# Sliding-window attention and a mixture of experts: the scores in TensorE tiles of 64 rows by 32 columns

## The chip, the core and the metric

The kernel runs on one core of a Trainium2 chip. The metric is device time in microseconds (us) of one execution. Before the change the median of three runs is 652.78 us (652.28 to 653.83). One execution was also taken by the hardware profiler: its own time is 656.34 us, and its span, from the first to the last instruction of the profile, is 654.3 us.

## What is computed

Attention with a causal window of 64 positions feeds a layer of eight experts, of which each token uses one. Cut to what matters here:

```python
B, H, S, D = 8, 8, 576, 64          # batch, heads, positions, head width; all float32
scores = q @ k.T / sqrt(D)          # per batch and head
rel = pos[:, None] - pos[None, :]
mask = (rel >= 0) & (rel < 64)      # a query sees itself and the 63 keys before it
attn = softmax(where(mask, scores, -1e9))
x = attn @ v                        # heads side by side: (B, S, 512)
...
e = argmax(x @ w_gate)              # or the expert of the position before, by a local gate
out = p[e] * (relu(x @ w1[e]) @ w2[e])
```

## The kernel before, in words

The 8 x 576 = 4608 positions are one row of tokens, cut into nine superblocks of 512 (`SC`, index `sc`). Heads are taken in pairs: `hp` counts four pairs, and `j` the two heads of a pair. A pair of `sc` and `hp` is a unit; there are 36, worked through in order.

Queries and keys lie with the 64 channels of a head on the partitions, head `j` on partitions 64j to 64j+63. Scores are made transposed: keys on the partitions of PSUM, queries along the columns. Keys come in blocks of 64. A PSUM bank (128 partitions by 512 float32) holds the scores of one head for the 512 queries of the unit: even key blocks in partitions 0 to 63 (`c` = 0), odd ones in 64 to 127 (`c` = 1). The 64 keys of a block can be seen by 128 queries, those of the block itself and of the next, so each matmul takes 64 keys as its stationary operand and streams 128 queries (64 at the two ends): `scores`, L376 to L420, with the matmul itself at L383. A unit has 18 such matmuls: in each head four even blocks of 128 queries, three odd ones of 128 and two odd ends of 64. Row half (head) and column half (`c`) make four tiles of 64 by 64 in TensorE's array. In the profile a float32 matmul is two weight loads (PEld, LDWEIGHTS) and two MATMUL records: 648 matmuls give 1296 of each.

ScalarE takes the exponential of the bank (L414) into an SBUF tile `p`, and VectorE multiplies it with a mask of zeros and ones (L419). In five of the 36 units (`BIASED`) there is no mask; instead small bfloat16 matmuls (L398) first write large negative numbers where a query doesn't see a key, and the score matmuls add to them (`start=False`). The banks come from a pool of three, `ps_s`, two for a unit.

`values` (L422 to L440) multiplies `p` with the values, in matmuls of 128 keys by 64 queries (L429), with a column of ones for the sum, and VectorE divides by that sum (L434, L439). Beside these, TensorE turns the results of some superblocks (L300) and computes gate logits (L313, L315, L330). A router works out the tables of the experts step by step between units (`step()`), on VectorE above all.

What sets the order: TensorE, ScalarE and SyncE run attention in the order in which the program writes it down (`manual_schedule`, L202). Scores are issued two units ahead of the values (`LEAD`, L475 and L501). SyncE (SP) issues the loads: queries and keys of a superblock (2 MB, L231) go into a ring of four 2 MB buffers, which is shared with the experts' weights (L1143), values (1.0 to 1.2 MB, L226) and, in the last five superblocks, values turned (1 MB, L221) go into buffers of their own. Loads are for the superblock after next, and each waits for its buffer to be released. GpSimd writes each superblock's result to DRAM (L529), some 1 MB. After attention the experts' stage runs to the end: gathered rows, two products per expert block (L1212, L1260, L1351, L1383) and scattered results, with small blocks in tiles of 128 by 32 (L1303, L1320).

Of the kernel before, what the change touches and what calls it, by code (L numbers as in the profile page):

```python
# [8 lines left out]
F32 = mybir.dt.float32  # L9
# [7 lines left out]
PSUM = bass.MemoryType.PSUM  # L17
DRAM = bass.MemoryType.DRAM

P = 128  # L20
B, H, S, DH = 8, 8, 576, 64
# [2 lines left out]
DK, FK = D // P, F // P  # L24
WIN = 64
KW = P + WIN
N = B * S
C = N // P
GB = 2
# [14 lines left out]
assert CUT and CUT % 32 == 0  # L44
LEFT = N - FB * BIG
HF = P // 2
NB = (N + E * (HF - 1)) // BIG
SM0 = NB * 2
# [10 lines left out]
SC = 4 * P  # L59
NSC = N // SC  # L60
HP = H // 2
KB = SC // WIN
# [19 lines left out]
def kernel(  # L82
# [20 lines left out]

    xs = dram.tile([N + 2, D], F32, name="xs")
    lt = const.tile([P, C, E + 1], F32, name="lt")
# [16 lines left out]
    with ExitStack() as fast:  # L122
        ring = fast.enter_context(tc.tile_pool(name="ring", bufs=4))
        rt = Router(fast, tc, lt, tabs, ident)
        ex = Experts(fast, tc, ring, *moe)
        zrow = ex.xp.tile([P, D], F32, name="xg")[:1]
        nc.vector.memset(zrow, 0.0)
        for i in (ZR, N + 1):
            nc.gpsimd.dma_start(out=xs[i:i + 1, :], in_=zrow)
        attention(tc, ring, kq, v3, v4, vt, vh, xs, lt, ok, wgs, wg2s, ident, rt, ex)  # L130
        ex.run(fast, rt, lambda ps: flag(nc, ps, ok, bad, tabs["ej"][:, NBLK:], rare, ident))
# [34 lines left out]
def attention(ctx, tc, ring, kq, v3, v4, vt, vh, xs, lt, ok, wg, wg2, ident, rt, ex):  # L166
# [14 lines left out]
    nc = tc.nc  # L181
# [3 lines left out]
    pp = ctx.enter_context(tc.tile_pool(name="at_p", bufs=LEAD + 3))  # L185
    wk = ctx.enter_context(tc.tile_pool(name="at_work", bufs=2))

    ps_s = ctx.enter_context(tc.tile_pool(name="at_ps_s", bufs=3, space=PSUM))
    ps_e = ctx.enter_context(tc.tile_pool(name="at_ps_e", bufs=1, space=PSUM))

    ps_x = [ctx.enter_context(tc.tile_pool(name=f"at_ps_x{i}", bufs=1, space=PSUM)) for i in range(2)]
# [8 lines left out]
        return ps_e.tile([P, SC], F32, name="r")  # L200

    ctx.enter_context(tc.manual_schedule(engines={ET.PE, ET.Activation, ET.SP}))  # L202

    kqs, qts, kts, vts, vas, vbs = {}, {}, {}, {}, {}, {}

# [169 lines left out]

    def scores(sc, hp):  # L376
        qt, kt = qts[sc], kts[sc]
        sp = [ps_s.tile([P, SC], F32, name="sp") for _ in range(2)]
        biased = (sc, hp) in BIASED

        def one(j, c, kt, block, a, b):
            h = slice(j * DH, (j + 1) * DH)
            nc.tensor.matmul(sp[j][c * WIN:(c + 1) * WIN, a:b], lhsT=kt[h, hp, block * WIN:(block + 1) * WIN],  # L383
                             rhs=qt[h, hp, a:b], start=not biased, stop=True, skip_group_check=biased)

        first = -sc * KB % SB
        if biased:
            for n in range(2):
                for c in range(2):
                    for j in range(2):  # L390
                        h, a = slice(j * DH, (j + 1) * DH), slice(0, SC)
                        x = bias[h, c].rearrange("p b i q -> p (b i q)")
                        if n:

                            if first >= KB or c == first % 2:
                                continue
                            a, x = slice(first * WIN, (first + 1) * WIN), never[h]
                        nc.tensor.matmul(sp[j][c * WIN:(c + 1) * WIN, a], lhsT=unit[h], rhs=x, start=not n, stop=False,  # L398
                                         skip_group_check=True)
        for s in range(5):  # L400
            for c in range(2):
                for j in range(2):
                    if c == 0:
                        if s < 4:
                            one(j, 0, kt, 2 * s, s * P, (s + 1) * P)
                    elif s:
                        one(j, 1, kt, 2 * s - 1, s * P - WIN, min(s * P + WIN, SC))
                    elif sc:
                        one(j, 1, kts[sc - 1], KB - 1, 0, WIN)
                    else:  # L410
                        one(j, 1, kt, 1, 0, WIN)
        p = pp.tile([P, 2, SC], F32, name="p")
        for j in range(2):
            nc.scalar.activation(p[:, j], sp[j], Act.Exp, scale=DH ** -0.5)  # L414
        if biased:
            return p
        a = 0 if sc == KB else (MID[sc % 2] - sc) * WIN
        m = masks[sc % 2][:, a:a + SC].rearrange("p (o x) -> p o x", o=1)
        masked.append(nc.vector.tensor_tensor(p, p, m.to_broadcast([P, 2, SC]), op=Alu.mult))  # L419
        return p  # L420
# [24 lines left out]
    for u in units[:LEAD]:  # L445
        ps[u] = scores(*u)
# [22 lines left out]
    for i, (sc, hp) in enumerate(units):  # L469
# [5 lines left out]
        if 1 < i < len(units) - LEAD:  # L475
            ps[units[i + LEAD]] = scores(*units[i + LEAD])
# [24 lines left out]
        if i < 2:  # L501
            ps[units[i + LEAD]] = scores(*units[i + LEAD])
# [32 lines left out]
    f = wk.tile([P, SC], F32, name="gs", bufs=1)[:, :NSC * 4 * H]  # L535
# [6 lines left out]
def careful(ctx, tc, q, k, v, xs, lt, wgs, ident):  # L542
# [15 lines left out]
    for cross in (False, True):  # L558
        m = cp.tile([P, 2, KW], F32, name=f"mask{int(cross)}")
        nc.gpsimd.memset(m, 0.0)  # L560
        nc.gpsimd.affine_select(out=m, in_=m, compare_op=Alu.is_ge, fill=NEG, base=-1,
                                pattern=[[0, 2], [1, KW]], channel_multiplier=-1)
        nc.gpsimd.affine_select(out=m, in_=m, compare_op=Alu.is_ge, fill=NEG, base=WIN,
                                pattern=[[0, 2], [-1, KW]], channel_multiplier=1)
        if cross:
            u = m[WIN:, :, :]
            nc.gpsimd.affine_select(out=u, in_=u, compare_op=Alu.is_ge, fill=NEG, base=-P,
                                    pattern=[[0, 2], [1, KW]], channel_multiplier=0)
        masks.append(m)
# [16 lines left out]
    def scores(st, half):  # L586
# [3 lines left out]
        for i in range(2):  # L590
            for j in range(2):
                h = slice(j * DH, (j + 1) * DH)
                nc.tensor.matmul(sp[:, j, i * KW + lo:(i + 1) * KW], lhsT=qt[h, 2 * half + i, t0:t0 + P],
                                 rhs=kt[h, 2 * half + i, t0 - WIN + lo:t0 + P], start=True, stop=True)
        s = wk.tile([P, 2, 2, KW], F32, name="s")
        mask = masks[st["c"] == CROSS]
# [938 lines left out]
```

## Time and profile before

| quantity | value |
|---|---|
| median of three runs | 652.78 us (652.28 to 653.83) |
| the profiled execution: its time, its span | 656.34 us, 654.3 us |
| PE busy, share of the span | 625.4 us, 96% |
| weight loads (PEld) busy | 538.5 us, 82% |
| VectorE, ScalarE, GpSimd busy | 402.2, 182.6, 124.4 us |
| records of PE and of PEld | 6307 each |
| score matmuls (L383): records, mean duration of one | 1296, 271 ns |
| value matmuls (L429): records, mean duration of one | 1152, 230 ns |
| exponentials (L414): count, mean | 72, 595 ns |
| first and last start of a score matmul | 5.3 and 133.9 us |
| data moved by DMA | 165.78 MB, mean 253 GB/s |

How to read it: PE rows are matmuls, PEld rows the loads of their stationary operand; both are TensorE. Matmuls are pipelined and last longer than the step from one to the next, so their busy times overlap, and the distance between starts says more than the duration. "Idle before" is time in which an engine stood still ahead of an instruction, with what ended the wait; "issue" there means that the profile knows of no wait. In the slices of the span each digit is the busy share of a fortieth of it (16.4 us), in tenths. The DMA queue that is called "instruction" brings the engines' instructions; the others carry data.

### The profile page before, as it was taken

To read this page: it belongs to the slowest core of one execution; us is meant where nothing else is said; L and a number is where in the kernel's file an instruction comes from. 1 tells how busy PE (TensorE), PEld (TensorE's weight loads), DVE (VectorE), ACT (ScalarE), POOL (GpSimd) and SP (SyncE) were. 2 spreads that over 40 slices of the span, in tenths; PEclk is the share of its full clock that TensorE was granted. 3 is DMA by queue.
4 is the path that set the end of the run, shared out by engine and by line. 5 is a ranking of instruction groups with operands and counts; after the bars stand their busy time and mean duration, and the time that the engine had idled before them with its cause. 6 is when DMAs were issued, how large, how long until landed. Compare 5 with 4: busy or idle time off the path is not lost. (4 is left out here: it accounts for less than half of the span.)

```text
span 654.3 us, 14680 instructions
## 1 busy us (share of the span) xinstructions
PE 625.4 (96%) x6307; PEld 538.5 (82%) x6307; DVE 402.2 (61%) x742; ACT 182.6 (28%) x318; POOL 124.4 (19%) x131
## 2 busy tenths in 40 slices
PE   8889887999999999999999999999999999999996
PEld 7777765786666899988799799978987998999994
DVE  5676479783996758336290876182835663876730
ACT  2866654621111221203121122113120322123220
POOL 5222111330104111121220311031222111101001
PEclk9999999999999999999999999999999999999998
DMA  9979989997436547566967845686858655945601
GB/s 337 400 292 395 362 311 361 371 357 277 161 128 216 204 160 262 204 218 248 374 244 264 310 174 185 263 304 264 339 183 307 241 198 180 386 165 190 245 17 39
DMA packets 21999, 165.78 MB, mean 253 GB/s; under 512 B 3453, under 2 KB 4483, under 8 KB 11940
## 3 DMA queue, kind: packets, MB, share of 16 engines
q1 hardware_dynamic: 13108, 135.24, 56.7%
q0 software_dynamic: 8816, 29.50, 11.4%
q8 instruction: 52, 0.85, 0.5%
q14 instruction: 23, 0.19, 0.1%
HBM read 145.85 MB, written 19.27 MB: 252 GB/s over the span
## 5 line engine op out<-in xcount | busy, mean ns | idle before, releaser
L1333 POOL DMA_INDIRECT out_dram<-y,idx x36 | 40.4, 1123 | 312.8 <-DVE y L1269 127.9
L1212 PE MATMUL hp<-xs,ws 128*128 128x128 f32 x672 | 79.7, 275 | 1.0 <-issue 1.0
L1212 PEld LDWEIGHTS hp<-xs,ws 128*128 128x128 f32 x672 | 77.3, 192 | 1.2 <-issue 1.2
L1260 PE MATMUL hp<-ws,hs 128*128 128x256 f32 x336 | 77.6, 380 | 0.0
L1260 PEld LDWEIGHTS hp<-ws,hs 128*128 128x128 f32 x336 | 63.5, 190 | 9.3 <-issue 0.8
L1351 PE MATMUL hp<-xt,w 128*64 128x64 f32 (+2 forms) x640 | 65.9, 275 | 0.0
L1269 DVE SCALAR_TENSOR_TENSOR y<-hp,pw,kept 128x256 f32<-128x256 f32 x42 | 19.7, 482 | 73.1 <-issue 48.7
L1351 PEld LDWEIGHTS hp<-xt,w 128*128 128x128 f32 (+1 forms) x640 | 60.8, 170 | 4.6 <-issue 1.1
L1223 DVE TENSOR_TENSOR h<-hp,keep 128x512 f32<-128x512 f32 x42 | 28.6, 690 | 54.0 <-PE hp L1212 46.7
L1131 POOL DMA_INDIRECT xg<-xs,gx x40 | 45.5, 1137 | 84.2 <-PE tp L1157 70.7
L1383 PE MATMUL yp<-w,h 128*128 128x512 f32 x128 | 56.2, 592 | 0.0
L1212 PEld LDWEIGHTS hp<-xt,w 128*128 128x128 f32 x448 | 53.2, 192 | 2.7 <-issue 1.3
L1212 PE MATMUL hp<-xt,w 128*128 128x128 f32 x448 | 54.7, 275 | 0.0
L1260 PE MATMUL hp<-w,h 128*128 128x256 f32 x224 | 53.6, 382 | 0.0
L419 DVE TENSOR_TENSOR p<-p,mask 128x1024 f32<-128x1024 f32 x31 | 39.1, 1265 | 20.7 <-ACT p L414 20.6
L414 ACT ACTIVATE p<-sp 128x512 f32<-128x512 f32 x72 | 39.1, 595 | 41.2 <-PE sp L383 39.1
L383 PEld LDWEIGHTS sp<-w 64*64 64x64 f32 x1296 | 38.7, 138 | 14.1 <-issue 10.7
L429 PE MATMUL xo<-vb,p 128*64 128x74 f32 (+1 forms) x576 | 44.8, 230 | 4.2 <-ACT p L303 1.5
L383 PE MATMUL sp<-w 64*64 64x128 f32 (+1 forms) x1296 | 44.2, 271 | 4.5 <-issue 3.6
L429 PE MATMUL xo<-va,p 128*64 128x74 f32 (+1 forms) x576 | 44.6, 230 | 3.4 <-DVE va L346 3.3
L429 PEld LDWEIGHTS xo<-vb,p 128*64 128x64 f32 x576 | 38.9, 138 | 8.5 <-issue 3.9
L1260 PEld LDWEIGHTS hp<-w,h 128*128 128x128 f32 x224 | 41.3, 190 | 5.6 <-issue 0.4
(284 smaller groups left out, 935.8 us busy)
## 6 DMA issues: line engine op xcount, KB each, us to landing
w<-in_w_dram SPq DMA_DIRECT2D x48, 2048.0 KB, 9.0
w<-in_kq_dram SPq DMA_DIRECT2D x17, 1024.0 KB, 10.5
xs<-x POOLq DMA_DIRECT2D x9, 1024.0 KB
va<-in_v_dram SPq DMA_DIRECT2D x5, 1184.0 KB
vtt<-in_vt_dram SPq DMA_DIRECT2D x5, 1024.0 KB, 6.7
va<-in_v_dram SPq DMA_DIRECT2D x3, 1040.0 KB, 8.0
va<-in_v_dram SPq DMA_DIRECT2D x2, 520.0 KB, 6.9
w<-in_kq_dram SPq DMA_DIRECT2D x2, 512.0 KB, 3.9
```

The lines of the kernel that those rows point to most:

```text
L383: nc.tensor.matmul(sp[j][c * WIN:(c + 1) * WIN, a:b], lhsT=kt[h, hp, block * WIN:(block + 1) * WIN], rhs=qt[h, hp, a:b], start=not biased, ...
L414: nc.scalar.activation(p[:, j], sp[j], Act.Exp, scale=DH ** -0.5)
L419: masked.append(nc.vector.tensor_tensor(p, p, m.to_broadcast([P, 2, SC]), op=Alu.mult))
L429: nc.tensor.matmul(xo[par * WIN:(par + 1) * WIN, j, s * VW:s * VW + n], lhsT=p[:, j, b * WIN:(b + 1) * WIN], rhs=w[:, s, 2 * hp + j, :n], ...
L1131: self.nc.gpsimd.indirect_dma_start(out=x, out_offset=None, in_=self.xs[:rows, :], in_offset=bass.IndirectOffsetOnAxis(ap=gx[:, s:s + 1], ...
L1212: nc.tensor.matmul(out[:, m, :], lhsT=a[:, kk, m * P:(m + 1) * P], rhs=b[:, kk, :], start=start and m + kk == 0, stop=stop and (m, kk) == ...
L1223: nc.vector.tensor_tensor(o, x, y, op=add)
L1260: nc.tensor.matmul(out, lhsT=a[:, m, :], rhs=b[:, m, :], start=start and m == 0, stop=stop and m == FK // 2 - 1, skip_group_check=True)
L1269: nc.vector.scalar_tensor_tensor(y[i][:, j * w:(j + 1) * w], x, pw[i], y2, Alu.mult, Alu.add)
L1333: self.nc.gpsimd.indirect_dma_start(out=self.out[:, :], out_offset=bass.IndirectOffsetOnAxis(ap=st["idx"][:, s:s + 1], axis=0), in_=y, in_ ...
L1351: nc.tensor.matmul(hp[a, i, :], lhsT=st["w1"][:, kk, m * P:(m + 1) * P][:, a], rhs=st["xt"][:, kk, :n], start=(kk == 0), stop=(kk == DK - 1))
L1383: nc.tensor.matmul(yp, lhsT=st["h"][:, m, i * P:(i + 1) * P], rhs=st["w2"][:, m, :], start=(m == 0), stop=(m == FK - 1))
```

## The change

The score matmuls are cut finer. The 64 keys of a block become two halves of 32 (`half`), each a matmul of its own into a tile of 64 rows by 32 columns. The first 32 keys of a block are seen by its own 64 queries and the first 32 of the next block, the other 32 from the 32nd query of their block on: each matmul now streams 96 queries in place of 128 (64 and 32 at the ends). A unit has 36 score matmuls in place of 18, in eight tiles in place of four. Part of each bank is then never written by a score matmul: those places hold scores that the mask sets to zero anyway. So that they hold finite numbers, the three banks are made once, zeroed by VectorE at the start, and taken in turn by `bank_s()`, in place of being allocated from the pool for each unit. The bias matmuls (L398), the exponential, the mask and the values are as before.

```diff
+HW = WIN // 2
...
-    ps_s = ctx.enter_context(tc.tile_pool(name="at_ps_s", bufs=3, space=PSUM))
+    ps_s = ctx.enter_context(tc.tile_pool(name="at_ps_s", bufs=1, space=PSUM))
...
+    sps = [ps_s.tile([P, SC], F32, name=f"sp{i}") for i in range(3)]
+    for sp in sps:
+        nc.vector.memset(sp, 0.0)
+
+    def bank_s():
+
+        sps.append(sps.pop(0))
+        return sps[-1]
...
-        sp = [ps_s.tile([P, SC], F32, name="sp") for _ in range(2)]
+        sp = [bank_s() for _ in range(2)]
         biased = (sc, hp) in BIASED
 
-        def one(j, c, kt, block, a, b):
-            h = slice(j * DH, (j + 1) * DH)
-            nc.tensor.matmul(sp[j][c * WIN:(c + 1) * WIN, a:b], lhsT=kt[h, hp, block * WIN:(block + 1) * WIN],
-                             rhs=qt[h, hp, a:b], start=not biased, stop=True, skip_group_check=biased)
+        def one(j, c, half, kt, block, own):
+
+            h, r = slice(j * DH, (j + 1) * DH), half * HW
+            q = slice(max(own + r, 0), min(own + r + WIN + HW, SC))
+            nc.tensor.matmul(sp[j][c * WIN + r:c * WIN + r + HW, q],
+                             lhsT=kt[h, hp, block * WIN + r:block * WIN + r + HW], rhs=qt[h, hp, q],
+                             start=not biased, stop=True, skip_group_check=biased)
...
         for s in range(5):
             for c in range(2):
-                for j in range(2):
-                    if c == 0:
-                        if s < 4:
-                            one(j, 0, kt, 2 * s, s * P, (s + 1) * P)
-                    elif s:
-                        one(j, 1, kt, 2 * s - 1, s * P - WIN, min(s * P + WIN, SC))
-                    elif sc:
-                        one(j, 1, kts[sc - 1], KB - 1, 0, WIN)
-                    else:
-                        one(j, 1, kt, 1, 0, WIN)
+                for half in range(2):
+                    for j in range(2):
+                        if c == 0:
+                            if s < 4:
+                                one(j, 0, half, kt, 2 * s, s * P)
+                        elif s:
+                            one(j, 1, half, kt, 2 * s - 1, s * P - WIN)
+                        else:
+                            one(j, 1, half, *((kts[sc - 1], KB - 1) if sc else (kt, 1)), -WIN)
```

## The prediction, as it was made

> **What bounds the kernel now.** I read the slices first. TensorE looks full in attention, its clock is granted in full, and the DMA engines are nearly full over the first seven slices (to about 115 us); later they are not.
>
> ```profile
> PE   8889887999999999999999999999999999999996
> ...
> PEclk9999999999999999999999999999999999999998
> DMA  9979989997436547566967845686858655945601
> ```
>
> Attention's steady stretch, 12 to 139 us, in the view by stages (columns: busy us of PE, PEld, DVE, ACT, POOL with record counts, clock, DMA share, GB/s):
>
> ```profile
> 12.00:139.00 127.00, 111.87 (x2635) 91.16 (x2633) 94.21 (x238) 74.43 (x126) 29.60 (x38) 0.99 0.93 353
> ```
>
> PE is busy 112 of 127 us; no other engine comes near. So PE's own work counts, but so do its 15 us of gaps. The waits of the score line say what ended its idle time, matmuls and weight loads together:
>
> ```profile
>   issue: 14.3, 15
>   ACT p L414: 2.4, 4
> ```
>
> "Issue" means that nothing the profile knows held the engine. The timeline shows such gaps in the middle of one unit's scores, where the next matmuls need no new data:
>
> ```profile
> 28.43 0.65 PE L383 MATMUL sp<-w 64*64 64x128 f32 x12
> 29.78 0.99 PE L383 MATMUL sp<-w 64*64 64x128 f32 x24 [0.70 <-issue]
> ...
> 75.64 1.09 PE L383 MATMUL sp<-w 64*64 64x128 f32 x28
> 78.55 0.55 PE L383 MATMUL sp<-w 64*64 64x128 f32 x8 [1.82 <-issue]
> ```
>
> I then numbered PE's records (weight loads and matmuls together). The gaps that no wait explains fall at numbers 705, 961, 1217, 2753, 3009, 4801 and 5313, all 193 plus a multiple of 256. They last 0.74, 0.70, 0.92, 0.15, 1.82, 1.08 and 0.34 us, 5.75 us in all. So it is the arrival of PE's instructions, in pages of 256. The page lists that queue (packets, MB, share of 16 engines):
>
> ```profile
> q8 instruction: 52, 0.85, 0.5%
> ```
>
> 0.85 MB over 52 packets is 16 KB each, 64 bytes for each of 256 instructions; 52 x 256 = 13,312 covers PE's 2 x 6307 records. By the single records, each page of attention has one such packet, lasting 0.9 to 1.7 us (mostly 1.0), and after every one of the seven gaps PE resumes 1.3 to 1.6 us after its end. The packet comes late: PE entered a page at 22.89 us, the packet for the next began at 27.33, ended at 28.40, and PE, out of instructions at 28.82, went on at 29.78. Taking a page's entry as the later of its arrival and the start of the record 64 earlier (the queue ahead of the array, see below), the wait from entry to packet in 20 pages averages 4.1 us in 17 (2.8 to 5.4), when loads were queued, and 1.1 to 1.4 us in three, when few or none were. So from request to use: 4.1 + 1.0 + 1.4 = **6.5 us** among loads, about 1.2 + 2.4 = **3.6 us** without. The stretch crosses 20 pages in 127 us, 6.35 us each, and by these times 13 of 20 pages arrived later than the queue could have taken them up. PE's instruction supply is a second bound, as tight as its matmuls.
>
> **What the Trainium skill says.** "Runtime: NRT & Kernel Launch", section "Instruction fetch mechanics": instruction memory is refilled in 16 KiB blocks of 256 instructions, the sequencer fetching the next while it executes the current one, and the crossing is mostly hidden. The trace agrees on the block and on one block ahead, and not on hidden: 5.75 us of gaps. "DMA: Bandwidth & Descriptors", section "Queues, rings and completion order": each DMA engine takes turns between queues, a packet at a time, so a fetch shares engines with loads; the 4.1 against 1.2 us fit. "TensorE: Matmul & The Clock Gate", section "Architectural detail": PE's queue holds 64 instructions; a gap shows only once it is empty, which fits that gaps are shorter than the lateness. "TensorEngine Tiling (Array Packing)", "Tiling Modes": 64x32 gives eight tiles that load and multiply independently, and changing the mode drains the array. No row has 64x32, but 128x32 with four tiles runs at full stream, and tiles start 7 ns apart:
>
> ```profile
> 318.20 1.95 PE L1320 MATMUL yp<-w,qt 128*32 128x128 f32 x64
> ```
>
> (64 passes over four tiles, 16 each, steps of 109 ns: 1.75 us and an end.)
>
> **The change, part by part.**
>
> *Fewer columns.* A float32 matmul is two passes, each a weight load and a matmul record (648 matmuls, 1296 records of each). In one tile the passes of 128 columns step by 109 ns, those of 64 by 56; 96 columns lie midway, 82 ns. A tile's eight passes of 128 (512 columns) become eight of 96: 8 x 27 = 0.21 us saved a unit, 7.7 us in 36 units. Eight tiles at 7 ns between starts need 56 ns a round, under 82, so the starts fit. If 64x32 doesn't stream so, this gain goes, and up to the present 0.90 us of a unit may double.
>
> *Twice the instructions.* Each unit issues 36 matmuls for 18, hence 72 weight loads and 72 passes for 36 and 36. In the stretch 1224 records of each kind belong to scores (34 units); 2448 are added to 5268: 7716, 30.1 pages for 20.6. Nothing else on PE is removed.
>
> *What that does to supply.* Work left per page is (111.9 - 7.3) / 30.1 = 3.5 us, against 5.4 now. A page among loads takes 6.5 us, so PE runs dry in nearly each. Loads occupy 44.9 MB (353 GB/s x 127 us) at some 395 GB/s, the rate of full slices: 113 us, however long the stretch is, since SP issues them when PE frees a buffer (SP's longest wait is for PE's L429, 40 us). During them 113 / 6.5 = 17.4 pages pass. The other 12.7 take the larger of 3.6 and 3.5 plus drains, 3.8 us: 48 us. The stretch becomes 161 us. The same sum on the kernel before gives 17.4 pages in 113 us and 3.2 at 5.4: 130 us against 127 measured. I take the difference of the two sums and the difference to the trace, 31 and 34, as +33 us. It already contains the 7.7 us: they shorten work that is no longer late.
>
> *Banks and zeros.* Three memsets of 512 columns on DVE; one such row takes 0.48 us, so they end near 2.9 us, ahead of the first scores at 5.33; ACT's table load, which now waits for them, ends near 4.2, ahead of the first exponential at 7.40. Nothing. Without that cover 1.4 us, once. The turn of three banks is the pool's own. In the five biased units the bias matmuls are 64x64 and the scores 64x32: five more drains of about 0.1 us, under the fetches.
>
> *Bounds and the rest.* If fetch delays among loads fall to 5.4 us since loads lie further apart, 113 / 5.4 = 20.9 pages and 9.2 x 3.8 = 35: 148 us, +18 to +21. If PE's clock halves in its idle spells (the trace has 0.83 in the stage 80 to 90 us, after the 1.82 us gap), the quiet pages cost 5.2: +18 us more. Later work keeps its length: first expert weights land about 14 us ahead of use, and from 139 us PE has 64 of 66 us busy.
>
> **Sum.** The profiled execution took 656.34 us (span 654.3), 3.6 over the median 652.78. 656.34 + 33 = 689; on the median 652.78 + 33 = 686; with a little for the clock, **687**.
>
> **Rivals.** (a) *Supply stays hidden* and the columns decide: 7.7 less 0.5 for drains, **645.6**. For it: most crossings show no visible gap. Against: pages come just in time now. It decides if a page among loads arrives within about 3.5 us. (b) *Two pages are requested at once* when PE runs dry, so delays overlap: a page costs (3.0 + 6.5) / 2 = 4.8, 23.5 pages in 113 us and 6.6 at 3.6: 137, +7 to +10, **661**. Against: after visible gaps the next packet comes 1.3 to 4.9 us after the resumption; counted from the last instruction before the gap it would be up to 6, longer than in the other pages. (c) *Starts limit eight tiles*: pairs no closer than today's 25 ns average make a unit 1.8 us. With fetches over much of it: **700**. Against: the 7 ns.
>
> **How the numbers follow.** Forecast 0.78 (668 to 710 by the bounds), (a) 0.07, (b) 0.10, (c) or a halved clock 0.05. The range 662 to 712 leaves out (a), half of (b) and the tails. A change of 0.2% is about what can be told here. Faster is (a): 0.07; same 0.02; slower 0.91.
>
> **What would show it.** Right: the instruction queue has 62 packets for 52; "issue" gaps of 1 to 4 us every 256 PE records in attention; PE busy share of the early slices falls to 5 or 6; loads get quiet spells; the stretch is some 33 us longer, the rest unchanged. Score passes stepping 82 ns with eight tiles shows the first part right. Wrong: as many gaps as now, or score units without gaps that last 1.3 us or more.

## The result, and the profile after

| | before | after |
|---|---|---|
| median of four runs, us | 652.53 (652.22 to 653.83) | 694.25 (691.42 to 696.60) |
| ratio, 95% interval | | 1.063 (1.060 to 1.066) |
| profiled execution: time, span, us | 656.34, 654.3 | 691.42, 689.6 |
| attention's stretch, us | 126.4 | 161.6 |
| TensorE records in the stretch, in pages of 256 | 5261, 20.6 | 7679, 30.0 |
| page gaps over 0.3 us: number, sum in us | 7, 7.5 | 18, 37.9 |
| TensorE at half clock in the stretch, us | 3.4 | 44.4 |

The stretch is counted here, and for all kernels below, from 12 us to the first TensorE record of the experts' first product (L1351 before, L1363 after; it is a wait, 0.7 us ahead of the first matmul). TensorE's records are its matmuls, its weight loads and its waits for semaphores, in the order of their starts. A page gap is the distance between the starts of two neighbouring records at a number of 193 plus a multiple of 256, if over 0.3 us.

The change costs 41.7 us in the medians and 35.1 us between the two profiled executions. The spans differ by 35.3 us, the stretches by 35.2. So the whole of what the profiles show was lost in attention, and 30.4 us of it are page gaps (37.9 for 7.5). The other 4.8 us aren't located. What follows it kept its length and its work, as the view by stages says of the kernel before (columns: stretch of time, its length, then busy us of PE, PEld, DVE, ACT, POOL with record counts, clock, DMA share, GB/s),

```profile
139.00:654.00 515.00, 504.42 (x3586) 439.07 (x3582) 302.50 (x493) 103.91 (x187) 88.69 (x79) 1.00 0.62 228
```

and of the kernel after, its attention first:

```profile
12.00:173.60 161.60, 122.67 (x3823) 98.59 (x3823) 90.81 (x236) 74.06 (x125) 29.99 (x38) 0.86 0.74 281
...
173.60:689.00 515.40, 504.81 (x3606) 439.66 (x3602) 302.71 (x494) 104.21 (x188) 86.05 (x79) 1.00 0.61 227
```

In the first line PE has 39 us without work where it had 15, its clock is 0.86 for 0.99, and the DMA engines, full before, stand still for a quarter of the time. The slices of the page show the same against the kernel before: PE's first ten digits fall from 7 to 9 to 6 to 8, the clock has dents among them, and the loads have quiet spells.

```profile
PE   7677777868999999999999999999999999999995
...
PEclk9689999898999999999999999999999999999998
DMA  9668777785835375556696676566966674854601
...
q8 instruction: 62, 1.02, 0.6%
```

The instruction queue brought 62 pages in place of 52. What ended the idle time ahead of the score matmuls, in the view of that line (us in all, times; the idle times of PE and PEld are added, so that most gaps count twice):

```profile
  issue: 60.6, 39
  ACT p L426: 3.0, 4
```

It was 14.3 us. The timeline shows where: in the middle of one unit's scores, which need nothing new. Columns are start, duration, instruction, count, and the idle time before it.

```profile
15.73 0.68 PE L395 MATMUL sp<-w 64*32 64x96 f32 x34
19.98 1.17 PE L395 MATMUL sp<-w 64*32 64x96 f32 x40 [3.57 <-issue]
...
151.69 0.37 PE L395 MATMUL sp<-w 64*32 64x96 f32 x12
156.27 1.49 PE L395 MATMUL sp<-w 64*32 64x64 f32 x60 [4.21 <-issue]
```

Both gaps stand at a page's border by the count of records. The packet of the missing page can be read beside them: the one for the second gap was asked for at 148.97 us, began 5.0 us later and lasted 0.9, and PE went on 1.4 us after it ended.

The zeroing of the banks, which the prediction priced at nothing, lies where it was put. ScalarE's table load waits for the first of the three banks and is done at 3.4 us, ahead of the first scores at 5.3:

```profile
1.57 1.57 DVE L207 MEMSET sp<- 128x512 f32 x3
2.14 1.28 ACT L426 ACT_TABLE_LOAD   x1 [2.14 <-DVE sp L207]
```

### The profile page after: what moved, and what is told of

It reads as the page before. It is cut to its first block, busy times and chain, and to the rows that moved or that the text cites. A ratio compares the mean times of both kernels' runs of the same rounds, so it can differ in the third digit from the quotient of the medians.

```text
span 689.6 us, 17285 instructions
## 1 busy us (share of the span) xinstructions
PE 636.3 (92%) x7603; PEld 546.2 (79%) x7603; DVE 401.4 (58%) x745; ACT 182.6 (26%) x318; POOL 121.9 (18%) x131
## 5 line engine op out<-in xcount | busy, mean ns | idle before, releaser
L1345 POOL DMA_INDIRECT out_dram<-y,idx x36 | 38.7, 1076 | 311.4 <-DVE y L1281 128.1
L395 PE MATMUL sp<-w 64*32 64x96 f32 (+2 forms) x2592 | 47.8, 265 | 25.5 <-issue 24.3
L395 PEld LDWEIGHTS sp<-w 64*32 64x32 f32 x2592 | 39.8, 117 | 39.7 <-issue 36.3
L1363 PE MATMUL hp<-xt,w 128*64 128x64 f32 (+2 forms) x640 | 65.9, 275 | 0.0
L1363 PEld LDWEIGHTS hp<-xt,w 128*128 128x128 f32 (+1 forms) x640 | 60.8, 170 | 4.6 <-issue 1.1
L441 PE MATMUL xo<-vb,p 128*64 128x74 f32 (+1 forms) x576 | 50.3, 247 | 9.6 <-issue 4.2
L441 PEld LDWEIGHTS xo<-vb,p 128*64 128x64 f32 x576 | 44.2, 153 | 17.4 <-issue 13.7
L441 PE MATMUL xo<-va,p 128*64 128x74 f32 (+1 forms) x576 | 50.1, 247 | 2.1 <-issue 2.1
```

The source lines that it names most:

```text
L395: nc.tensor.matmul(sp[j][c * WIN + r:c * WIN + r + HW, q], lhsT=kt[h, hp, block * WIN + r:block * WIN + r + HW], rhs=qt[h, hp, q], start=n ...
L441: nc.tensor.matmul(xo[par * WIN:(par + 1) * WIN, j, s * VW:s * VW + n], lhsT=p[:, j, b * WIN:(b + 1) * WIN], rhs=w[:, s, 2 * hp + j, :n], ...
L1345: self.nc.gpsimd.indirect_dma_start(out=self.out[:, :], out_offset=bass.IndirectOffsetOnAxis(ap=st["idx"][:, s:s + 1], axis=0), in_=y, in_ ...
L1363: nc.tensor.matmul(hp[a, i, :], lhsT=st["w1"][:, kk, m * P:(m + 1) * P][:, a], rhs=st["xt"][:, kk, :n], start=(kk == 0), stop=(kk == DK - 1))
```

## The experiments

Two theories were held against each other. *Supply*: the added instructions make TensorE wait for its instruction pages, which come slowly while loads are moving. *Array*: eight tiles of 64 by 32 load and multiply slower than four of 64 by 64, and the time is lost inside a unit's scores. In e2, e3, e8 and e12 scores are missing or others than asked for. This changes the routing, extra paths of the program then run, and their total times of 1016 to 1059 us say nothing. Only attention's stretch is used of them; the total times that were expected of e2 and e3 can't be compared. e8, e9 and e12 were executed once each. The stretch varies from execution to execution: kernels that keep the instruction count of before give 122.7 to 126.4 us.

| kernel | stretch, us | TensorE records, pages | page gaps: number, us | at half clock, us | time over before |
|---|---|---|---|---|---|
| e1: 64x64, queries cut in two | 156.5 | 7138, 27.9 | 14, 28.1 | 27.3 | 1.049 (1.044 to 1.054) |
| e2: 64x32, half of the keys | 126.4 | 5256, 20.5 | 8, 12.5 | 10.2 | |
| e3: 64x64, one head of two | 120.3 | 4032, 15.8 | 2, 3.0 | 6.8 | |
| e4: banks alone | 122.7 | 5197, 20.3 | 9, 8.8 | 3.4 | 1.003 (1.001 to 1.005) |
| e5: after, loads in 2 KB | 165.8 | 7671, 30.0 | 22, 42.7 | 41.0 | 1.060 (1.054 to 1.066) |
| e6: before, loads in 2 KB | 126.1 | 5215, 20.4 | 7, 6.5 | 10.2 | 1.004 (1.002 to 1.005) |
| e8: after, half of the q and k loads | 155.6 | 7644, 29.9 | 16, 33.6 | 27.3 | |
| e9: after, loads in 16 KB | 163.2 | 7622, 29.8 | 18, 38.0 | 41.0 | one run: 692.76 us |
| e10: before, 18 small matmuls a unit more | 163.5 | 7341, 28.7 | 13, 23.2 | 20.5 | 1.059 (1.051 to 1.067) |
| e11: before, 9 small matmuls a unit more | 143.1 | 6325, 24.7 | 12, 11.1 | 3.4 | 1.030 (1.024 to 1.035) |
| e12: after, 8 queries a matmul | 163.9 | 7686, 30.0 | 19, 41.2 | 68.3 | |
| e13: before, 72 empty instructions a unit more | 267.3 | 7821, 30.6 (2492 of them empty) | 0 | 97.5 | 1.214 (1.209 to 1.219) |

### Tile shape or instruction count: e1 and e2

e1 keeps the kernel before with its tiles of 64 by 64 and cuts each score matmul of 128 queries in two:

```diff
-            nc.tensor.matmul(sp[j][c * WIN:(c + 1) * WIN, a:b], lhsT=kt[h, hp, block * WIN:(block + 1) * WIN],
-                             rhs=qt[h, hp, a:b], start=not biased, stop=True, skip_group_check=biased)
+            for q in range(a, b, WIN):
+                nc.tensor.matmul(sp[j][c * WIN:(c + 1) * WIN, q:q + WIN],
+                                 lhsT=kt[h, hp, block * WIN:(block + 1) * WIN],
+                                 rhs=qt[h, hp, q:q + WIN], start=not biased, stop=True, skip_group_check=biased)
```

> The kernel before, with its tiles of 64 by 64 and all its columns, but each score matmul of 128 queries is cut into two of 64: 32 matmuls a unit in place of 18, the columns the same. Attention's stretch then has 5268 + 34 x 56 = 7172 instructions on TensorE, 28.0 pages. Theory of instruction supply: the changed kernel took 39 us more for 9.5 pages more, 4.1 us a page, so 7.4 pages more cost 30 us: 683 us (675 to 690), with unexplained gaps at every 256th record. Rival, that tiles of 64 by 32 themselves are slow: no such tile here, so 652 to 658 us. Rival, that only columns count: 652.5 to 654 us.

Measured: 687.66 us, 1.049 times before; the stretch is 156.5 us. No tile is finer than before, no column is added, and yet 30 of the 35 us are there. The finer cut has an array cost of its own, though: a unit without a gap takes 1.204 us from first to last start (29.78 to 30.98 here),

```profile
29.78 1.42 PE L384 MATMUL sp<-w 64*64 64x64 f32 x64
```

and 0.900 before (14.68 to 15.58):

```profile
14.68 1.12 PE L383 MATMUL sp<-w 64*64 64x128 f32 x36
```

In 34 units that is up to 10 of the 30 us. The page gaps grew by 20.6 us. e2 is the other half, the changed kernel with the first 32 keys of each block alone, so that the old instruction count meets the new tiles:

```diff
-                for half in range(2):
+                for half in range(1):
```

> The changed kernel, but only the first 32 keys of each block are multiplied (half = 0); the other half of the scores is left out, and those places keep zeros or the bias. 18 matmuls a unit, as many instructions as the kernel before, all in tiles of 64 by 32 with 96 queries. Supply theory: 20.6 pages in the stretch as before, and 0.2 us less work a unit that mostly only widens the gaps: 650 us (644 to 654). Rival, that the tile shape is slow: the shape is used in every unit, so half of the loss or more stays: 670 us or more.

Measured: a stretch of 126.4 us, equal to before. Together they say that the time goes with the count more than with the tiles. e2 has half of the matmuls, in four tiles at a time, so it doesn't tell how eight tiles work together; the units of the changed kernel itself do, under e12.

### Fewer instructions, and the banks alone: e3 and e4

Both take from the change only the banks that are made once and zeroed. e3 also leaves out the scores of the second head (`for j in range(1)` in the loop of the score matmuls).

> The kernel before with its three banks made once and zeroed, and the score matmuls of the second head of each pair left out (its banks keep what was in them). The two tiles that are left still stream 512 columns each, so the array is occupied as long as before, with half the score instructions: 5268 - 1224 = 4044 in the stretch, 15.8 pages. Supply theory, that already the kernel before is held by its pages: the gaps of 5.75 us go and late pages hold nothing: 645 us (641 to 648). Rival, that the kernel before is bound by its columns alone and supply bound only the changed one: 651.5 to 653.5 us.

Measured: 15.8 pages in place of 20.6, two page gaps for seven, and a stretch that is 6 us shorter than before. e3 has the banks of e4, though, and against e4 it is 2.4 us shorter, less than the 3.7 us by which kernels of one count differ. That the kernel before lost a little to its supply is seen in its own seven gaps; what their absence gains e3 doesn't show.

> One part of the change alone: the three banks made once, zeroed at the start and taken in turn, with the matmuls of the kernel before. All theories: nothing, 652.5 us (651.5 to 653.5). If the turn of the banks or the memsets had a share in the loss, it would show here.

Measured: 656.11 us, 1.003 (1.001 to 1.005), a little above the expected range. The profiled execution doesn't contain the difference (its span of 652.2 us is 2.1 below the one of before), so it isn't located. It is at most 3 us of the 41.7.

### The same count with little to multiply: e12

The changed kernel, each score matmul cut to its first 8 queries; most scores are left out.

```diff
-            q = slice(max(own + r, 0), min(own + r + WIN + HW, SC))
+            q = slice(max(own + r, 0), max(own + r, 0) + 8)
```

> The changed kernel with each score matmul cut from 96 queries to the first 8: the same 36 matmuls a unit in the same eight tiles, so the same instruction count, with a twelfth of the streaming. Most scores are left out, so the routing is another and only attention's stretch is to be compared. Theory (count and supply decide): 157 to 162 us, as the changed kernel's 161.6, with as many late pages. Rival (the array's work in eight tiles costs the time): the stretch falls by what a unit's scores shrink, 34 x 0.3 to 0.5 us = 10 to 17 us, to 145 to 151 us.

Measured: 163.9 us, as the changed kernel. Whole units without a gap show that the array's work did shrink. A unit's scores after,

```profile
32.94 1.07 PE L395 MATMUL sp<-w 64*32 64x96 f32 x72
```

and in e12:

```profile
53.86 0.78 PE L395 MATMUL sp<-w 64*32 64x8 f32 x72
```

From first to last start, a clean unit (no gap, full clock) takes 0.612 us and not 0.867; in 34 units that is 8.7 us of array work less, and nothing of it shows in the stretch. What ended the idle time ahead of e12's score line is almost what it was after:

```profile
  issue: 57.7, 42
```

The stretch of e12 alone doesn't refute the array theory. e12 ran 68 us at half clock, 24 more than the changed kernel, and that can have made up for the 8.7 us: by the prediction's rule for a page's entry, TensorE didn't wait for 7 of its 30 pages, and five of these 7 follow a page worked through mostly at half clock. So e12 doesn't settle either what the half clock was worth.

Two readings of the changed kernel decide. Its 16 clean units of scores take 0.867 us each, where a clean one took 0.900 before: in eight tiles a unit is no slower, and there is nothing for the array theory to explain. And by the same rule 26 of its 30 pages (13 of 20 before) began only when their packet had come, at every gap 1.2 to 1.6 us after the packet's end.

### Count added to the kernel before: e10, e11 and e13

e10 sends ahead of each score matmul, in units without bias, one of 8 queries into the same place; e11 does so for the first head alone (`if not biased and j == 0`).

```diff
         def one(j, c, kt, block, a, b):
             h = slice(j * DH, (j + 1) * DH)
+            if not biased:
+                nc.tensor.matmul(sp[j][c * WIN:(c + 1) * WIN, a:a + 8], lhsT=kt[h, hp, block * WIN:(block + 1) * WIN],
+                                 rhs=qt[h, hp, a:a + 8], start=True, stop=True)
```

> The kernel before (64x64 tiles, 128 queries), with an added matmul of 8 queries ahead of each score matmul, whose result the score matmul overwrites; in the 31 units without bias matmuls. That is the instruction count of the changed kernel almost in full (some 7350 in the stretch, 28.7 pages) with next to no array work added. Theory (count of instructions, supplied among loads at 6.5 us a page and else at 3.8): 17.4 pages in 113 us and 11.3 x 3.8 = 43 us, 156 us by the sum that gave 130 for the 126 to 127 us of before: a stretch of 152 to 156 us, time 678 to 684 us. Rival (the array's work in eight finer tiles costs the time): 127 to 130 us and 653 to 656 us.

> The same with the added matmuls for the first head of each pair alone: half of the added instructions (some 6300 in the stretch, 24.6 pages). Theory: 17.4 pages in 113 us and 7.2 pages at their own work of 4.55 us, 33 us: 146 by the sum, 142 to 146 in the trace, time 668 to 673 us. Rival (there is slack up to some count, and only the full count goes beyond it): 127 to 132 us, time 653 to 658 us.

Measured: 694.17 and 672.54 us, stretches of 163.5 and 143.1. (One of e10's four executions took 1768 us, for a cause that no trace shows. The ratio leaves it out; the other three took 689.9 to 695.4 us.) e10 overshot its expectation, and its units show why that can be: from first to last start a clean one takes 1.736 us and in e11 1.628, for 0.900 before. The small matmuls were not next to nothing; each brings two weight loads and two passes more. Over 29 units that is 24 us in e10 and 21 in e11, where the stretches grew by 37 and 17 and the page gaps by 15.7 and 3.6. e10 and e11 therefore don't separate the theories. e11's hit on the number of the supply theory is no support for it.

e13 wanted the added count with no array work: four empty instructions ahead of each score matmul, 2592 in all, as many as the change adds.

```diff
         def one(j, c, kt, block, a, b):
             h = slice(j * DH, (j + 1) * DH)
+            for _ in range(4):
+                nc.tensor.nop(hint="keep", nofuse=True)
```

> The kernel before with four empty instructions (no operation) on TensorE ahead of each score matmul: 2592 added in attention, exactly as many as the change adds, and no work on the array at all. Theory (count and supply): the stretch becomes 152 to 162 us, time 678 to 694 us, the instruction queue has 62 packets, and the late pages come every 256 instructions with the empty ones counted. Rival (array work in finer tiles): 126 to 130 us and 652 to 656 us. Second rival (the empty ones are slow by themselves): the time is lost inside each unit of scores and not at the pages.

Measured: 794.8 us. The second rival of its expectation is what happened. A unit's scores last up to 5.59 us, and none of the 30 page borders in the stretch shows a gap:

```profile
22.10 5.59 PE L385 MATMUL sp<-w 64*64 64x128 f32 x36
```

The same 36 passes lasted 1.12 us before. The empty instructions have records, too: 2592 of them, two thirds of which start 70 or 71 ns after the one before. A page then lasts 8.7 us on average, and the next one has all the time it needs. The run confirms one number only: its instruction queue brings 62 packets, as after, so empty instructions fill pages as others do.

### Why a page takes so long: e5, e6, e9 and e8

The prediction had the fetch wait for load packets on a shared DMA engine. If it is packets that it waits for, their size must matter. e5 cuts the loads of the changed kernel into rows of 2 KB for queries and keys (8 KB before), and the values likewise; e6 does the same to the kernel before; e9 loads queries and keys in rows of 16 KB, from the second superblock on.

```diff
-                nc.sync.dma_start(out=vts[sc], in_=vt[GATED.index(sc)])
+                for hp in range(HP):
+                    nc.sync.dma_start(out=vts[sc][:, hp], in_=vt[GATED.index(sc)][:, hp])
...
-                nc.sync.dma_start(out=vas[sc][:, :, h], in_=src[:, :, h])
+                for c in range(4):
+                    nc.sync.dma_start(out=vas[sc][:, c, h], in_=src[:, c, h])
...
-                nc.sync.dma_start(out=kqs[sc][:, part], in_=kq[sc, :, part])
+                for hp in range(part.start, part.stop):
+                    for i in range(2):
+                        nc.sync.dma_start(out=kqs[sc][:, hp, i], in_=kq[sc, :, hp, i])
```

> The changed kernel with its loads of queries, keys and values cut finer: queries and keys in rows of 2 KB and not of 8 KB in one partition, values per four-way chunk, turned values per head pair; the same bytes, more DMAs, the same TensorE instructions. Theory (an instruction page waits behind a number of load packets already queued on its DMA engine, whose size sets the wait): the wait from request to packet among loads falls from about 3.8 us towards 2 us, the attention stretch from 162 us to 130 to 140 us, the time to 660 to 675 us. Rival (the wait is set by bytes in flight, or by something other than the loads): the wait stays near 3.8 us, the stretch near 160 us and the time near 694 us. Second rival (the added issues on SP delay the loads themselves): ScalarE and TensorE waits for loads appear and the time is above 694 us.

> The kernel before with the same finer loads. Theory (wait behind load packets): its seven page gaps of 7.5 us vanish and the time falls to 645 to 649 us. Rival (wait not set by the size of the packets): 652 to 653 us as before.

e9, from the changed kernel:

```diff
+            elif sc and part.start:
+                continue
             else:
+                part = slice(0, HP) if sc else part
                 if sc not in kqs:
```

> The changed kernel with queries and keys of a superblock loaded in one DMA of 2 MB, rows of 16 KB in one partition in place of two DMAs with rows of 8 KB. Theory (number of packets ahead times their size): the wait among these loads grows from about 3.8 us towards 6 us, the stretch from 162 to 175 to 190 us. Rival (bytes in flight, or not the loads): 160 to 164 us.

Measured: 694.21, 656.48 and 692.76 us. The expectations of this theory failed in all three. The load packets did change: their mean durations from 12 to 160 us were 92 ns in e5, 304 after and 394 in e9. The waits didn't. I sorted the pages of the stretch by whether the DMA engines were over 45% busy from the request to the packet:

| kernel | pages among loads: number, wait us, us to the next request | pages in quiet: number, wait us, us to the next request |
|---|---|---|
| before | 18, 3.75, 6.30 | 1, 1.11, 5.48 |
| after | 21, 3.59, 5.86 | 8, 1.42, 4.12 |
| e1 | 19, 4.03, 6.31 | 8, 1.37, 3.95 |
| e5, 2 KB | 24, 3.52, 5.83 | 5, 1.33, 4.02 |
| e9, 16 KB | 21, 3.70, 6.00 | 8, 1.28, 4.04 |
| e8, half of the q and k loads | 15, 3.90, 6.23 | 14, 1.38, 4.05 |
| e12 | 22, 3.49, 5.91 | 7, 1.37, 3.92 |

The averages of the two classes stand apart in every kernel: 3.5 to 4.0 us and 1.1 to 1.4 us. Single waits among loads spread widely, from 1.4 to 5.8 us after. So a page does come later on average while loads move, and between rows of 2 and of 16 KB it doesn't matter in what pieces they move. e8 then takes loads away: the first two head pairs of queries and keys are loaded and used for all four, in packets as large as before; the scores are therefore partly others.

```diff
+            elif part.start >= HP // 2:
+                continue
             else:
                 if sc not in kqs:
...
-                             lhsT=kt[h, hp, block * WIN + r:block * WIN + r + HW], rhs=qt[h, hp, q],
+                             lhsT=kt[h, hp % 2, block * WIN + r:block * WIN + r + HW], rhs=qt[h, hp % 2, q],
```

> The changed kernel with only the first two head pairs of queries and keys loaded and used for all four: half of the query and key loads, some 9 MB of 47 in the stretch, are left out, with packets as large as before. Scores of half of the heads are therefore others than asked for, and the routing with them, so that only attention's stretch is to be compared. Theory (pages wait only while loads are queued): loads occupy 38 MB / 395 GB/s = 96 us in place of 120, so 3.7 fewer pages wait 6.5 us and the stretch falls by about 10 us, from 162 to about 152. Rival (the wait is not the loads'): 162 us, as the changed kernel.

Measured: 155.6 us, 6 less than after, where about 10 was expected. Six pages passed from the slow class into the quick one, and the two classes nearly kept their times. By the table that is 15 x 6.23 + 14 x 4.05 = 150 us for after's 21 x 5.86 + 8 x 4.12 = 156: the 6 us. That loads are what delays a page is thus supported by taking them away, in a single execution; how they delay it isn't shown. A wait that is set by the bytes in flight, the rival in e5's expectation, fits e5, e6 and e9 and wasn't tested further. The records don't say which DMA engine carries a page, so what exactly is ahead of it stays open.

Nothing tried here points to a version that is faster than the kernel before. Finer loads (e6) and banks made once (e4) are 0.3 to 0.4% slower, and all else that was tried adds instructions or leaves work out.

## Why the prediction was right, point by point

- *The bound.* Right. After the change attention is limited by TensorE's instruction supply: 30.4 of the 35.2 us are page gaps, clean units are no slower, and e1 and e2 show the count from two sides. The pages of 256, one ahead, and the resumption some 1.4 us after a packet's end were read from the kernel before and held after.
- *Twice the instructions.* 7716 records and 30.1 pages were forecast for the stretch, 7679 and 30.0 came.
- *Supply.* The stretch was to be 161 us and is 161.6, but the terms of that sum were off in opposite directions. "During them 113 / 6.5 = 17.4 pages pass" was mis-sized: 21 pages passed among loads, in 123 us, at 5.86 each. The loads move the same bytes, but at least one engine was busy with data for 131.5 us (123.9 before), so that 113 us from the rate of full slices was too short; and the wait was 3.6 us for the 4.1 forecast (3.75 in the kernel before itself, by the sorting used above). "The other 12.7 [...] 3.8 us: 48 us" became 8 pages of 4.12, 33 us. The incomplete pages at the two ends make up the remaining 5.6 us. The hit on 161 is partly luck.
- *The range's end at "fetch delays among loads fall to 5.4 us".* The measured 5.86 lies between that and 6.5, but with more pages in that state.
- *Why loads delay a page.* The prediction took from the Trainium skill ("DMA: Bandwidth & Descriptors", "Queues, rings and completion order") that a DMA engine takes turns between queues by packets, and found that the waits of 4.1 and 1.2 us fit. Pieces of 2, 8 and 16 KB gave 3.52, 3.59 and 3.70 us. The two classes are real, but the wait doesn't follow the size of the records in the trace, and this reading of the section isn't supported. The section itself isn't refuted: by a packet it means a group of descriptors, and no run shows how the records map to these.
- *"Mostly hidden"* ("Runtime: NRT & Kernel Launch", "Instruction fetch mechanics"): 18 of 30 page borders of the changed kernel show a gap, 37.9 us in all. The sentence doesn't hold for a stream of small matmuls among loads.
- *Fewer columns.* Wrong, at no cost. "Eight tiles at 7 ns between starts need 56 ns a round, under 82, so the starts fit" failed. A clean unit goes from 0.900 to 0.867 us from first to last start, 0.03 us saved and not 0.21. In e2, with four tiles of 64 by 32 and 96 queries, the same eight passes a tile take 0.660 us: that is the 82 ns step, and the 0.24 us. So the width streams as supposed, and eight tiles don't run at it together: 72 weight loads and 72 passes in 0.867 us are 12 ns a pair, where 7 were assumed, and even with 8 queries (e12) a pair takes 8.5 ns. What holds the pairs apart isn't shown. Had supply stayed hidden, rival (a) would have had 1 us to gain and not 7.7.
- *Banks and zeros.* Nothing, in the trace; at most the 3 us of e4's interval.
- *The half clock.* The prediction allowed up to 18 us for it. 44 us of the stretch ran at half clock, far more than was seen before, but a page in quiet cost 4.12 us for 3.8, some 0.3 x 8 = 2.6 us. And all that isn't page gaps grew by 4.8 us, so by this sum the clock can hardly have cost more than that. The timeline of the changed kernel has such a unit, at half clock and with the DMA engines 42% busy while its page was waited for; it lasts 1.69 us and not 1.07, and its page took 4.8 us from request to request:

```profile
27.76 1.69 PE L395 MATMUL sp<-w 64*32 64x96 f32 x72
```

- *The sum.* 687 forecast, 694.25 measured. On the profiled executions the step is 35.1 us where 33 was forecast. The other 6.6 us of the medians' 41.7 come from which execution was profiled: the one of before lies 3.8 us above its median, the one of after 2.8 below. What a longer execution of the changed kernel does otherwise, no trace shows.
- *The signs.* 62 packets, gaps at every 256th record (18 of 30 borders) and quiet spells of the loads came as named. PE's busy share in the early slices fell to 6 to 8 and not to 5 or 6, and the passes don't step by 82 ns in eight tiles.
- *The rivals.* (a) supply hidden: no, 18 gaps. (b) two pages requested at once: no, requests follow each other by 4 us at least on average, and one packet at a time comes. (c) starts limit eight tiles: in part, but at 0.867 us a unit and not 1.8, and it isn't what the time goes to.

## What to carry to other kernels

Count TensorE's instructions before cutting matmuls finer: in float32 each matmul here is two weight loads and two passes, and a page of 256 instructions took some 4 us to be replaced in quiet and 6 us while loads moved. In this kernel the work in a page became shorter than that, the time went with the instruction count, and fewer columns didn't show. The sign in a profile is idle time by "issue" in the middle of a run of like matmuls, at every 256th record, with more packets in the instruction queue.

## What was not expected of the hardware

- The wait for an instruction page among loads is the same with load rows of 2, 8 and 16 KB (3.52, 3.59, 3.70 us on average), and 1.1 to 1.4 us in quiet.
- Empty instructions on TensorE follow one another by 71 ns, some six times as long as a weight load and a pass of a full unit in eight tiles (12 ns).
- A matmul of 8 queries ahead of one of 128 in the same tile isn't free: 18 of them lengthen a unit's scores from 0.900 to 1.736 us. Nor is it free to cut one of 128 queries in two: a unit then takes 1.204 us.
- Seven spells at half clock, 44 us in all, in the changed kernel's stretch, where the kernel before had one of 3.4 us.
